# Attention and routed experts on one core: a new order for the swaps, the first pairs, the first plan and the last pairs

## The chip, the core and the metric

The kernel runs on one core of a Trainium2 chip. Its engines have queues of their own: TensorE (PE in the profile, its weight loads PEld), VectorE (DVE), ScalarE (ACT), GpSimd (POOL), and SyncE (SP), which here only issues transfers. Transfers run on the core's 16 DMA engines. The metric is the device time of one execution in microseconds (us), as the median of the runs. In the profile L230 is line 230 of the kernel.

## What is computed

Attention over 8 batches of 8 heads (576 tokens, 64 columns a head), with rotary positions on q and k, and behind it a layer of 8 experts in which each token goes to the one with the highest gate:

```python
q_rot, k_rot = (rotate(q), rotate(k))
scores = scale * np.matmul(q_rot, k_rot.transpose(0, 1, 3, 2))
attn = softmax(scores)
x = (attn @ v)                      # as (4608 tokens, 512)
...
logits = x @ w_gate + modality_bias[modality_id]
e_idx = np.argmax(logits, axis=1)
for e in range(8):
    mask = e_idx == e
    h = np.maximum(x[mask] @ w1[e], 0.0)
    out[mask] = gate_w[mask, None] * (h @ w2[e])
```

## The kernel before, in words

**Attention** goes by 32 pairs of heads, four pairs to a batch. The loop over the pairs (L734) doesn't emit work directly: each step is a job with a key (`KEYS`, in us within a pair's period `PER` = 14.438), jobs are sorted by key + `PER` x pair (L819), and each engine, SP too, runs its share strictly in that order. So a smaller key means an earlier place in an engine's queue, not a time. Negative keys belong to pairs ahead. The steps of a pair:

- LD (`load`, L139): q and k of the pair, with the rotated partner beside them, 1216 columns, into one of two stages `Rs`. SP issues it; it has to wait until the pair two before has been read by LO.
- T1, T2, R (`rope_` parts 0 to 2, L230, L232, L234): two products with the cosine and sine tables and their sum, on GpSimd for pairs from 2 on, on VectorE for pairs 0 and 1.
- HI (L221 by way of `acopy`, ScalarE) rounds the result to the matmul's type; LO (L238, GpSimd) is what rounding left. Each matmul of the scores runs as three: high x high, low x high, high x low.
- SWH and SWL (`swap`, L246): a copy of the high and of the low part, `SW`, in which the two heads have changed halves of the partitions; two transfers of 64 partitions each, so four a pair. SWH has its key behind HI, SWL behind LO.
- S0 to S8 (`scores`, L261), MN (`rowmin`, L270) and EX (`expo`, L277): score tiles on TensorE into a ring of three PSUM buffers, the row minimum on VectorE, the exponential on ScalarE into `PJ` and `P4`.
- F0 to FB (`fill`, L283; evacuated by `evac`, L315 or L221): transposes of the exponentials into `PH` and `PD`.
- AVA, AVB (L339), OUTA, OUTB (L370), EVA, EVB (L384 to L390): times V, back to rows of tokens with the gate's logits beside them, and division by the row sum.
- LV (`loadv`, L147, L148): V of the pair, four transfers.

The keys that matter here, from `KEYS`: T1 -32.78, T2 -26.38, R -23.03, HI -18.83, SWH -17.41, LO -15.27, SWL -11.79, LD -39.33, LV -10.14, S8 -5.22. Modulo the period this gives on GpSimd the order T1 of the next pair, LO of this one, T2 and R of the next; and on SP: SWL of a pair, LD of the pair two on, LV.

**Routing** comes once in four pairs, in 13 steps (`route`, keys `AT["rk"]`) over ScalarE, VectorE, GpSimd and TensorE. Then five scatters (`scatter`, L472, GpSimd's queue) write each token's number and weight to its rank in the table `TAB`; their keys lie 10.5 apart (9.0 in one batch). XO (L395, L399) writes the batch's rows to `X`.

**The first plan** (`plan(0)`, L479) runs after six batches, in 28 steps. From the counts so far it takes eight full blocks of 256 tokens with one expert each, so that the expert layer can start before the last two batches are routed. It works on one partition, on GpSimd, with its sums and one shift (L492) on VectorE.

**The experts** go by blocks (`chain`, L845): table rows (`m_ix`, L604, L606), gathers of X (L614, GpSimd), transposes (L655), weights W1 and W2 into `ST1` and `ST2` (L626, L631, SP; these are also the stages `Rs` and the tables), split into high and low parts (L218, L221), 96 matmuls for W1 (L673) and 48 for W2 (L690), and a scatter of the result (L694). For block 0 this work is put among the last pairs by keys counted from pair 31 (`Z`, L786 to L818). W2's two parts (`mw`, L825) and the experts' PSUM banks are allocated after attention's pools have been closed (L824), and wait for all of them.

**The start**: pair 0 comes in three pieces of columns, `FIRST` (L151): 0 to 416, 928 to 1216, 416 to 928. Each goes through all five steps of the rotation and its swaps before the next. Pair 1's load is issued behind them (L157), its rotation follows on VectorE, then the loads for pairs 2 and 3, V, and `setup2` (L202: the modality bias, on GpSimd). Only then do the sorted jobs begin.

## Time and profile before

| | us |
|---|---|
| median of 3 runs | 976.48 |
| lowest, highest | 976.05, 978.91 |
| the profiled execution | 978.22 |
| its span, first to last instruction | 976.4 |
| first score matmul | 14.86 |
| first matmul with W1 | 524.08 |
| first matmul with W2 | 550.96 |

The profile is one execution of the program. Its timelines give the start of an instruction, its length, engine, line, the tile that it writes and the ones that it reads, and in brackets how long the engine had been idle ahead of it and what ended that. Merged rows have a count behind an x. A row of SPq is the issue of a transfer, not the transfer. Windows give for a stretch its length and each engine's busy time; then the clock that TensorE was granted, the mean busy share of the DMA engines, and GB/s. The view of waits gives who waited for whom: us in total, how often, and the longest. Busy TensorE isn't TensorE at its best: matmuls overlap, and a slower clock makes them longer.

### The profile page before, as it was taken

The page shows a single profiled execution, that of the slowest core. Times are in us where ns is not written, and L with a number is a line of the kernel's source. Part 1 is how long each engine was busy: PE and PEld are TensorE (multiplying, and loading weights), DVE is VectorE, ACT ScalarE, POOL GpSimd, SP SyncE. Part 2 cuts the span into 40 slices and gives each one's busy share as a digit, 9 for nine tenths or more (in the row PEclk, how much of TensorE's full clock was granted, in tenths as well). Part 3 has the DMA queues.
Part 4 walks back from the last instruction along what each step waited for, and adds up shares of the span by engine and source line. Part 5 has one row for each costly group of instructions (what it writes and reads, how often), then busy time and mean ns, then how long its engine had stood idle before and what let it go on. Part 6 is the DMA issues. An engine that isn't in the chain of part 4 may idle for free. (4 is left out here: it accounts for less than half of the span.)

```text
span 976.4 us, 24969 instructions
## 1 busy us (share of the span) xinstructions
PE 908.2 (93%) x9248; PEld 742.4 (76%) x9248; DVE 674.2 (69%) x1158; ACT 632.3 (65%) x1299; POOL 663.8 (68%) x498
## 2 busy tenths in 40 slices
PE   1899999999999999989977899999999999999996
PEld 1677677777777767767646689999998888899995
DVE  6677777787777777777754478677666666666771
ACT  1778787787787877868753355666555656556661
POOL 7776788889878798799656076557666666556500
PEclk9799999999999999999989899999999999999998
DMA  9645667566574755746751261111431611611100
GB/s 285 194 142 173 180 198 221 148 188 202 174 225 134 201 185 175 228 130 182 207 149 34 64 211 36 55 48 58 142 120 42 218 38 45 227 44 49 41 24 15
DMA packets 71964, 132.71 MB, mean 136 GB/s; under 512 B 28395, under 2 KB 48267, under 8 KB 66844
## 3 DMA queue, kind: packets, MB, share of 16 engines
q1 hardware_dynamic: 61436, 110.32, 37.8%
q0 software_dynamic: 9536, 19.48, 6.4%
q8 instruction: 75, 1.23, 0.6%
q10 hardware_dynamic: 864, 1.25, 0.4%
q14 instruction: 53, 0.43, 0.2%
HBM read 140.59 MB, written 19.77 MB: 164 GB/s over the span
## 5 line engine op out<-in xcount | busy, mean ns | idle before, releaser
L270 DVE TENSOR_REDUCE mn<-ps 128x1 f32<-128x576 f32 x288 | 205.4, 744 | 104.2 <-PE ps L261 67.3
L277 ACT ACTIVATE P<-ps,mn 128x576 f32<-128x576 f32 x288 | 210.4, 737 | 97.6 <-DVE mn L270 90.4
L614 POOL DMA_INDIRECT XG<-X,iy x152 | 180.9, 1190 | 47.5 <-issue 41.4
L673 PE MATMUL psH<-HL,W1H 128*128 128x256 f32 x1152 | 202.7, 279 | 0.0
L261 PE MATMUL ps<-HL 64*128 64x288 f32 x960 | 170.7, 315 | 29.8 <-ACT HL L221 14.9
L261 PE MATMUL ps<-SW 64*128 64x288 f32 x960 | 170.3, 316 | 9.0 <-DMA SW<-HL 4.7
L261 PEld LDWEIGHTS ps<-HL 64*128 64x128 f32 x960 | 137.7, 190 | 53.2 <-ACT P L277 15.9
L673 PEld LDWEIGHTS psH<-HL,W1H 128*128 128x128 f32 x1152 | 176.8, 188 | 1.7
L673 PE MATMUL psH<-HL,W1L 128*128 128x256 f32 x576 | 160.8, 279 | 0.7 <-DVE W1L L218 0.7
L261 PEld LDWEIGHTS ps<-SW 64*128 64x128 f32 x960 | 135.4, 190 | 24.4 <-ACT P L277 14.1
L218 DVE TENSOR_TENSOR W1L<-ST,W1H 128x1024 fp32r<-128x1024 f32 x76 | 90.0, 1222 | 84.6 <-ACT W1H L221 82.6
L339 PE MATMUL pa<-PH,V 128*64 128x320 f32 (+1 forms) x1024 | 142.2, 420 | 1.1 <-PE ps L261 0.7
L694 POOL DMA_INDIRECT out_dram<-y,ix x38 | 39.1, 1030 | 143.6 <-ACT y L693 129.8
L690 PE MATMUL psY<-W2H,SW 128*128 128x512 f32 x304 | 120.3, 396 | 1.4 <-ACT W2H L221 1.4
L690 PE MATMUL psY<-W2L,SW 128*128 128x512 f32 x304 | 120.4, 396 | 0.4 <-DVE W2L L218 0.4
L283 PE MATMUL ps<-idf,P 64*128 64x64 f32 x2624 | 105.3, 229 | 8.8 <-DVE PH L315 2.4
L283 PEld LDWEIGHTS ps<-idf,P 64*128 64x128 f32 x2624 | 92.6, 141 | 22.7 <-ACT PH L221 8.6
L315 DVE COPY PH<-ps 128x512 f32<-128x512 f32 (+1 forms) x160 | 97.3, 632 | 17.4 <-PE ps L283 10.9
L339 PEld LDWEIGHTS pa<-PH,V 128*64 128x64 f32 x1024 | 69.8, 139 | 51.5 <-issue 14.5
L673 PEld LDWEIGHTS psH<-HL,W1L 128*128 128x128 f32 x576 | 108.2, 188 | 0.9 <-DVE W1L L218 0.9
L221 ACT ACTIVATE PH<-ps 128x512 f32<-128x512 f32 (+1 forms) x160 | 84.0, 556 | 22.1 <-PE ps L283 14.9
L218 DVE TENSOR_TENSOR W2L<-ST,W2H 128x1024 fp32r<-128x1024 f32 x76 | 92.4, 1220 | 4.1 <-ACT W2H L221 3.6
(159 smaller groups left out, 1602.9 us busy)
## 6 DMA issues: line engine op xcount, KB each, us to landing
ST<-in_moe_w_dram SPq DMA_DIRECT2D x152, 512.0 KB
ST<-in_qk_dram SPq DMA_DIRECT2D x31, 1216.0 KB
SW<-HL SPq DMA_DIRECT2D x124, 232.0 KB
V<-in_v_dram SPq DMA_DIRECT2D x64, 128.0 KB
X<-X SPq DMA_DIRECT2D x8, 1024.0 KB
XG<-X,iy POOLq DMA_INDIRECT x152
V<-in_v_dram SPq DMA_DIRECT2D x64, 16.0 KB
X<-XT SPq DMA_DIRECT2D x32, 32.0 KB
```

The costliest lines, as they stand in the source:

```text
L218: nc.vector.tensor_tensor(o, a, b, op=ALU.subtract)
L221: return nc.scalar.activation(o, i, AF.Copy, scale=scale)
L261: free(nc.tensor.matmul(ps[:, g, 0:288], t[:, wq, q0:q0 + P], t[:, wk, k0:k0 + 288], start=(m == 0), stop=(m == len(L) - 1)), seen)
L270: lastmin[d["ring", u]] = nc.vector.tensor_reduce(mn, d["S", u][:, :, 0:288], op=ALU.min, axis=AX.XY).ins
L277: nc.scalar.activation(p.rearrange("p (a b) -> p a b", a=2), ps[:, :, 0:288], AF.Exp, bias=d.pop(("m", u)), scale=-1.0, accum_out=d["sum"] ...
L283: free(nc.tensor.transpose(ps[0][:, g, c:c + 64], src[r, k0:k0 + P], idf[r, r]), ps[1])
L315: mine.append((nc.vector.tensor_copy if g else acopy)(o, i).ins)
L339: nc.tensor.matmul(pa[hh * 64:hh * 64 + 64, 0:c1 - c0], d["V"][:, hh, kt, :], r, start=(kt == 0), stop=(kt == 4))
L614: nc.gpsimd.indirect_dma_start(out=XG[s % 2][:, t, g, :], out_offset=None, in_=X.rearrange("n (i f) -> (n i) f", f=P)[0:rows], in_offset=b ...
L673: nc.tensor.matmul(ps[:, i, :], w[:, c, f0:f0 + P], x[:, c, :], start=(m == 0), stop=(m == 11))
L690: nc.tensor.matmul(ps, hx[:, c, t * P:(t + 1) * P], w[:, c, :], start=(m == 0), stop=(m == 23))
L694: nc.gpsimd.indirect_dma_start(out=out, out_offset=bass.IndirectOffsetOnAxis(ap=d["ix"][:, t, 0:1], axis=0), in_=y, in_offset=None, bounds ...
```

## The change

- `swap` sends both parts in one transfer, so there are two a pair, at SWL's key. SWH is no longer used. For pair 0 the second transfer of each piece goes out on ScalarE's queue.
- `FIRST` becomes 0 to 288, 672 to 1216, 288 to 672. The rotation of the three pieces is interleaved. The score tiles of pair 0 come in the order 8, 6, 7, 0 to 5; its evacuations follow their transposes directly, and AVA and AVB come directly behind the last transposes.
- Pair 1's load is issued behind the first piece's swap; its rotation runs on GpSimd, with HI, LO and the swap behind pair 0's transposes F3. Behind these come the load of pair 3 and T1, T2, R of pair 2. `setup2` goes to key 20.5.
- The route steps from the fourth on are moved later, up to 33.0. Scatters lie 2.5 apart and no longer wait for one another.
- `plan0`, a generator of nine steps, replaces `plan(0)`. It counts full blocks by comparisons and a sum, without the shift; sums on VectorE, the rest on GpSimd. It starts at the tenth route step.
- The first plan's table reads and the scatters of the last two batches no longer wait for each other.
- Block 0's side work has new keys. W2's parts take the places of `PJ` and `PH` as soon as these are done with, and are split during pair 31, not behind it. Pools of the experts wait by tile, not for all of attention.
- V's main parts of both heads come in one transfer. `y` and `BT` have places of their own.

```diff
 AT = dict(
-    rk=(0, 0.6, 1.5, 4.7, 5.5, 6.3, 6.9, 7.5, 9.6, 10.4, 11.2, 14.4, 15.2),
-    pl=1.5,
-    sc=(10.5, 9.0),
-    tr=3.5,
-    te=-8.0,
-    hi=(-14.0, -9.0, -5.0, -1.0),
+    rk=(0, 0.6, 1.5, 7.0, 8.5, 9.5, 10.0, 11.0, 24.0, 24.9, 25.6, 32.0, 33.0),
+    pl=(0.5, 6.5, 7.5, 13.5, 14.5, 20.5, 21.5, 28.5, 29.5),
+    sc=2.5,
+    plan=(-30.5, -21.0, -14.5, -13.0, 2.0, 4.0, 6.0, 8.0),
+    ix=(-19.7, -12.5, 0.0, 5.0),
+    rows=(-15.0, -4.0, 6.5),
+    gap=(1.35, 1.3, 1.3),
+    w1=(-29.3, -27.8, -23.2, -20.9),
+    w2=(-8.5, -6.5, -4.0, -1.5),
+    te=(-4.0, -2.0),
+    hi=(-14.0, -10.0, -6.0, 0.0),
+    hi2=(10.2, 11.4, 12.6, 13.8),
+    lo2=(17.0, 18.2, 20.8, 22.0),
     l1=(7.0, 10.0, 13.7, 17.6),
     l1e=3.0,
-    sp2=(0.2, 0.4, 1.4, 1.8),
-    l2=2.0,
-    w1=(1.0, 5.7, 8.0, 10.2),
-    w2=(-8.0, -5.0, -2.0, 1.0),
-    plan=(-99.0, -15.0, 4.0, 6.0, 8.0, 10.0, 12.0, 14.0),
-    ix=(-16.5, -9.5, 4.0, 6.0),
-    rows=4.0,
-    gap=1.3,
+    l2=0.1,
...
-    pp = att.enter_context(tc.tile_pool(name="pp", bufs=1))
+    pp = ctx.enter_context(tc.tile_pool(name="pp", bufs=1))
...
+    W2 = [None] * 2
+    places = [ExitStack(), ExitStack()]
+
+    def place(i, name, **kw):
+        return places[i].enter_context(tc.tile_pool(name=name, bufs=1, reuse_waits="tile", **(dict(side="right") if i == 0 else {}), **kw))
+
+    def weights2(i):
+        places[i].close()
+        W2[i] = ctx.enter_context(tc.tile_pool(name=f"w2{i}", bufs=1, reuse_waits="tile", **(dict(side="right") if i == 0 else {}))).tile(
...
+    pj = place(0, "pj")
+    PJ = [pj.tile([P, 2 * S], F32, name=f"P{j}") for j in range(4)]
...
     def loadv(n):
         b, hp = divmod(n, 4)
         V = Vs[n % 2]
+        nc.sync.dma_start(out=V[:, :, 0:4, :].rearrange("p h j d -> p h (j d)"),
+                          in_=v[b, 2 * hp:2 * hp + 2, 0:512, :].rearrange("h (p j) d -> p h (j d)", j=4))
         for hh in range(2):
-            src = v[b, 2 * hp + hh]
-            nc.sync.dma_start(out=V[:, hh, 0:4, :], in_=src[0:512, :].rearrange("(p j) d -> p j d", j=4))
-            nc.sync.dma_start(out=V[hh * 64:hh * 64 + 64, hh, 4, :], in_=src[512:576, :])
-
-
-    FIRST = ((0, 416), (K1, QW), (416, K1))
...
+    FIRST = ((0, Q0), (672, QW), (Q0, 672))
     st[0] = dict(R=Rs[0], HL=HL[0], SW=SW[0], V=Vs[0])
     for c0, c1 in FIRST:
         nc.sync.dma_start(out=Rs[0][:, :, c0:c1], in_=qk[0, :, :, c0:c1])
         nc.scalar.dma_start(out=COS[:, c0:c1], in_=rope[0, :, c0:c1])
         nc.scalar.dma_start(out=SIN[:, c0:c1], in_=rope[1, :, c0:c1])
...
-        BT = PJ[0][:, 0:B * 5 * E].rearrange("p (b e) -> p b e", e=E)
...
-        e = nc.vector if n < 2 else nc.gpsimd
...
-    def swap(n, i, c0=0, c1=QW):
+    def swap(n, c0=0, c1=QW, engs=None):
         d = st[n]
         a, b = (d[t].bitcast(F32) for t in ("SW", "HL"))
         for g in range(2):
             c = slice(max(c0, Q0 * g), min(c1, QW if g else K1))
             if c.start < c.stop:
-                nc.sync.dma_start(out=a[g * 64:g * 64 + 64, i, c], in_=b[64 - g * 64:128 - g * 64, i, c])
...
+    placed = []
+    taken = []
+
     def scatter(b, j):
         oi = bt_[b]["oi"]
         n = P if j < 4 else 64
-        nc.gpsimd.indirect_dma_start(
+        inst = nc.gpsimd.indirect_dma_start(
             out=TAB, out_offset=bass.IndirectOffsetOnAxis(ap=oi[0:n, j:j + 1], axis=0),
-            in_=VAL[0:n, b, j, :], in_offset=None, bounds_check=E * N - 1, oob_is_err=False)
+            in_=VAL[0:n, b, j, :], in_offset=None, bounds_check=E * N - 1, oob_is_err=False).ins
+
+        for _b, x in placed:
+            tc.declare_no_dep(inst, x, reason="rows of other tokens")
+        placed.append((b, inst))
+        if b >= B - 2:
+            for x in taken:
...
+    def plan0():
+        G_ = nc.gpsimd
...
+        def total(o, i):
+            nc.vector.tensor_reduce(o, i, op=ALU.add, axis=AX.X)
+
+        most = (B - 2) * S // BLK
+        sl = cview("SL")[0:1]
+        nf, nb, cum, ge, tk = (t1(x, [E]) for x in ("nf", "nb", "cum", "ge", "tk"))
+        G_.tensor_tensor(nf, RUN[0:1, B - 2, :], cview("EB")[0:1], op=ALU.subtract)
+        th = t1("th", [NB_MAX])[:, 0:most]
+        G_.tensor_scalar(th, sl[:, 0:most], float(BLK), float(BLK), op0=ALU.mult, op1=ALU.add)
+        full = t1("full", [E, NB_MAX])[:, :, 0:most]
+        sh = [1, E, most]
+        G_.tensor_tensor(full, nf.unsqueeze(2).to_broadcast(sh), th.unsqueeze(1).to_broadcast(sh), op=ALU.subtract)
+        G_.tensor_scalar(full, full, 0.0, None, op0=ALU.is_ge)
+        yield
+        total(nb, full)
+        t88 = t1("t88", [E, E])
+        G_.tensor_tensor(t88, cview("TRI")[0:1].rearrange("p (a b) -> p a b", b=E), nb.unsqueeze(1).to_broadcast([1, E, E]), op=ALU.mult)
+        yield
+        total(cum, t88)
+        yield
+        sh = [1, NA, E]
+        cmp = t1("cmp", [NB_MAX, E])[:, 0:NA, :]
+        G_.tensor_tensor(cmp, cum.unsqueeze(1).to_broadcast(sh), sl[:, 0:NA].unsqueeze(2).to_broadcast(sh), op=ALU.subtract)
+        G_.tensor_scalar(cmp, cmp, 0.0, None, op0=ALU.is_le)
+        es = t1("pes", [NB_MAX + 1])
+        G_.memset(es[:, 0:1], -1.0)
+        yield
+        total(es[:, 1:NA + 1], cmp)
+        yield
+        G_.tensor_scalar(es[:, 1:NA + 1], es[:, 1:NA + 1], float(E - 1), None, op0=ALU.min)
+        G_.tensor_copy(PLA[:, 0, 0:NA], es[:, 1:NA + 1])
...
+        G_.tensor_scalar(ge, nb, -float(BLK), float(N), op0=ALU.mult, op1=ALU.add)
+        G_.tensor_tensor(cmp, cmp, ge.unsqueeze(1).to_broadcast(sh), op=ALU.mult)
+        yield
+        rb = t1("rb", [NB_MAX])[:, 0:NA]
+        total(rb, cmp)
...
+        i1 = nc.sync.dma_start(out=ix, in_=TAB[bass.ds(d["r"], BLK), :].rearrange("(p t) w -> p t w", t=2)).ins
         xi = d["xi"] = ixp.tile([P, 8, 2], I32, name="xi", tag="xi")
-        nc.sync.dma_start(out=xi, in_=TAB[bass.ds(d["r"], BLK), :].rearrange("(q g) w -> q (g w)", g=8).unsqueeze(0).to_broadcast([4, 32, 16]))
+        i2 = nc.sync.dma_start(out=xi, in_=TAB[bass.ds(d["r"], BLK), :].rearrange("(q g) w -> q (g w)", g=8).unsqueeze(0).to_broadcast([4, 32, 16])).ins
+        if not slots[s][0]:
+            for i in (i1, i2):
+                for b, x in placed:
+                    if b >= B - 2:
+                        tc.declare_no_dep(i, x, reason="the first plan's blocks lie before the rows of the last two batches")
...
-    for n in range(2):
-        for c in FIRST if n == 0 else ((0, QW),):
-            for part in range(5):
-                rope_(n, part, *c)
-                if part > 2:
-                    swap(n, part - 3, *c)
-        load(n + 2)
-    for n in range(2):
-        loadv(n)
-    setup2()
+
+    for part, c in ((0, 0), (1, 0), (2, 0), (3, 0), (4, 0), (0, 1), (1, 1), (2, 1), (3, 1), (0, 2), (4, 1), (1, 2), (2, 2), (3, 2), (4, 2)):
+        rope_(0, part, *FIRST[c])
+        if part == 4:
+            swap(0, *FIRST[c], engs=(nc.sync, nc.scalar))
+        if (part, c) == (4, 0):
+            load(1)
+    loadv(0)
+    load(2)
+    loadv(1)
+    for part in range(3):
+        rope_(1, part)
     z = NPAIR - 1
     end = max(K["EVA"], K["EVB"]) + 0.015
     r0 = end + 0.005
+
+    places_ = sorted(range(9), key=lambda u: K[f"S{u}"])
+    first = (8, 6, 7, 0, 1, 2, 3, 4, 5)
+    OV = {0: {}, 1: {}, 2: {}}
+    for nm in ("S", "MN", "EX"):
+        OV[0].update({f"{nm}{u}": K[f"{nm}{w}"] for u, w in zip(first, places_)})
+    full = max(K[f] for f in K if f[0] in "SF") + 0.05
+    assert full + 0.3 < min(K[f"S{u}"] for u in range(9)) + PER
+    for f in ("F0", "F1", "F2", "F3", "FA", "FB"):
+        OV[0].update({f"{e}_{f}": K[f] + 0.01 for e in "AB"})
+    OV[0].update(AVA=full + 0.01, AVB=full + 0.02)
+    for i, nm in enumerate(("HI", "LO", "SWL")):
+        OV[1][nm] = K["F3"] + 0.02 + 0.01 * i - PER
+    for i, nm in enumerate(("T1", "T2", "R")):
+        OV[2][nm] = K["F3"] + 0.1 + 0.01 * i - 2 * PER
+    J(K["F3"] + 0.06, "load", 0, load, 3)
...
+        if n > 0:
+            for part, nm in enumerate(("T1", "T2", "R", "HI", "LO")):
+                if n > 1 or part > 2:
+                    K_(nm, rope_, n, part)
+            K_("SWL", swap, n)
         if n > 1:
-            for part, nm in enumerate(("T1", "T2", "R", "HI", "LO")):
-                K_(nm, rope_, n, part)
-            for i in range(2):
...
+            if n == NPAIR - 9:
+                g = plan0()
+                for i in range(9):
+                    J(r0 + AT["rk"][9] + AT["pl"][i], "plan", n, next, g, None)
             for j, (f, *a) in enumerate(scats):
...
+    for s in range(NA):
+        Z(A["plan"][s], m_plan, s)
+    for s in range(4):
+        Z(A["ix"][s], m_ix, s)
+    for s in range(3):
+        for i in range(8):
+            Z(A["rows"][s] + A["gap"][s] * i, m_gather, s, i // 4, i % 4)
...
+        Z(A["w1"][g], m_load1, 0, g)
+        Z(A["w2"][g], m_load2, 0, g)
+        Z(A["hi"][g], m_hi, 0, g)
+        Z(A["hi"][g] + 1.3, m_lo, 0, g)
+        if g == 0:
+            for i in range(2):
+                Z((A["hi2"], A["lo2"])[i][0] - 0.01, weights2, i)
+        Z(A["hi2"][g], m_hi, 1, g)
+        Z(A["lo2"][g], m_lo, 1, g)
+    for t in range(2):
+        Z(A["te"][t] - 0.5, m_tr, 0, t)
...
-        Z(end + A["sp2"][g], m_split, 1, g)
...
-    mw = ctx.enter_context(tc.tile_pool(name="mw", bufs=1))
-    W2[0] = mw.tile([P, 8, DM], F32R, name="W2H")
-    W2[1] = mw.tile([P, 8, DM], F32R, name="W2L")
-    W2[2] = ctx.enter_context(tc.tile_pool(name="my", bufs=2))
     for kind, nb in (("H", 4), ("Y", 4)):
-        banks[kind] = ctx.enter_context(tc.tile_pool(name=f"ps{kind}", bufs=nb, space=PSUM))
```

More of the change, by code (lines that the diff above doesn't have):

```diff
@@ L483, in t1, with plan @@
+    def plan():
+        V_ = nc.vector
+        pl, ns = PLB, NB_MAX
         def t1(name, sh, dt=F32):
@@ L765, in tile_attention_moe @@
             g = route(n // 4)
-            early = n == NPAIR - 9
             r1 = r0 + AT["rk"][-1] + 0.02
@@ L813, in tile_attention_moe @@
-    for g in range(4):
-        l1 = max(A["l1"][g], A["hi"][g] + 1.5, w1_ + 11.5, te_[1] + 1.5, max(K[f] for f in K if f[0] in "SF") + 0.1 * g + 0.1)
+    planned = r0 + AT["rk"][9] + AT["pl"][-1] - 8 * PER
+    assert A["ix"][0] > r1 + 4 * AT["sc"] - 8 * PER
+    fills = max(K[f] for f in K if f[0] in "SF")
+    assert A["plan"][0] > planned and A["ix"][0] > planned and A["w1"][0] > max(K["T1"], K["LO"] - PER)
+    assert A["w2"][0] > max(K["T2"], K["LO"]) and A["te"][0] > max(K[f"S{u}"] for u in range(9)) - PER
```

126 lines of the change are left out of this document (52 added, 74 removed).

## The prediction

> **What bounds the kernel now.** I read the page first, then the stages by windows, then the timeline of single queues. The page's row of TensorE over 40 slices of the span, busy tenths in each:
>
> ```profile
> PE   1899999999999999989977899999999999999996
> ```
>
> TensorE is the bound nearly everywhere, and what it loses lies in the first slice and in slices 21 to 23, where attention hands over to the experts. Windows by stage (length, busy time of each engine, granted clock, DMA share, GB/s): one attention pair, the handover, and a block of the experts.
>
> ```profile
> 53.27:67.88 14.61, 14.45 (x205) 10.82 (x203) 10.90 (x24) 11.55 (x32) 11.17 (x5) 1.00 0.57 173
> 496.07:550.96 54.89, 40.91 (x359) 29.86 (x359) 22.86 (x46) 20.60 (x46) 27.42 (x28) 0.84 0.29 74
> 573.80:598.70 24.90, 24.90 (x164) 22.54 (x163) 17.41 (x25) 14.12 (x18) 16.85 (x16) 1.00 0.33 112
> ```
>
> The expert block is full, as are its neighbours in the row of slices: nothing is to be had there, and the change leaves them alone. In attention a pair takes 14.6 us where nothing disturbs it, and TensorE is busy for 14.45 of them. So a second loop matters, one that is only just hidden: GpSimd and SP at work on the rotation. GpSimd's timeline for one turn, then SP's:
>
> ```profile
> 190.26 2.79 POOL L238 TENSOR_TENSOR HL<-ST,HL 128x1216 fp32r<-128x1216 f32 x1
> 193.00 2.78 POOL L232 TENSOR_TENSOR ST<-ST 128x1216 f32<-128x1216 f32 x1
> ...
> 200.81 2.80 POOL L230 TENSOR_TENSOR ST<-ST 128x1216 f32<-128x1216 f32 x1 [1.06 <-DMA ST<-in_qk_dram]
> 203.55 2.81 POOL L238 TENSOR_TENSOR HL<-ST,HL 128x1216 fp32r<-128x1216 f32 x1
> ```
>
> ```profile
> 188.41 5.76 SPq L246 DMA_DIRECT2D SW<-HL  x4
> 194.23 0.57 SPq L139 DMA_DIRECT2D ST<-in_qk_dram  x1
> ```
>
> LO (L238) of one pair ends at 193.0; SP then sends the low half's swap and the load two pairs on (LD, 194.23); T1 (L230) of that load waits for it; the next LO stands behind that T1. From LO to LO that is 203.55 - 190.26 = 13.3 us, against TensorE's 14.6. T1 waits for its load 25 times, as the view of waits says; in an undisturbed pair LO in the end waits 1.2 us for ScalarE:
>
> ```profile
> POOL ST L230 <- DMA ST<-in_qk_dram: 51.1, 25, 3.9
> ```
>
> ```profile
> 53.21 2.78 POOL L238 TENSOR_TENSOR HL<-ST,HL 128x1216 fp32r<-128x1216 f32 x1 [1.21 <-ACT HL L221]
> ```
>
> So the loop's slack is 14.6 - 13.3 = 1.3 us.
>
> **The change, part by part.** Times are of the profiled execution: 978.2 us, of which its span is 976.4; the median of the runs shown is 976.48, so I add differences to 976.5.
>
> *One transfer for both halves of a swap.* It removes two of four SP issues for each pair. But the high half, so far sent while LO still ran, now goes with the low half after LO, and LD stands behind both in the same queue. The high half alone, in one-microsecond windows:
>
> ```profile
> 189.00:190.00 1.00, 1.00 (x14) 0.64 (x12) 0.87 (x2) 1.00 (x5) 1.00 (x1) 1.00 0.50 112
> 190.00:191.00 1.00, 1.00 (x12) 0.61 (x10) 0.00 (x0) 1.00 (x4) 1.00 (x2) 1.00 0.94 215
> 191.00:192.00 1.00, 1.00 (x18) 0.83 (x16) 0.32 (x1) 0.07 (x1) 1.00 (x1) 1.00 0.54 177
> ...
> 195.00:196.00 1.00, 1.00 (x18) 0.95 (x16) 0.50 (x1) 0.80 (x3) 0.84 (x2) 1.00 0.99 299
> ...
> 197.00:198.00 1.00, 1.00 (x26) 0.80 (x24) 1.00 (x4) 1.00 (x5) 1.00 (x1) 1.00 1.08 428
> ```
>
> The shares of the first three rows add up to 0.50 + 0.94 + 0.54 = 1.98, so a half (128 rows of 928 floats, 475 KB) takes 2.0 us of all sixteen engines. At 299 GB/s it would take 1.6, at 428 (the load's best row) 1.1; nothing if the load could pass it. I take 1.8, near its own rows. The loop becomes 13.3 + 1.8 = 15.1 us, longer than TensorE's 14.6: **GpSimd, SP and the queue become the bound of attention**.
>
> A rule speaks for the transfer. The Trainium skill, "DMA: Bandwidth & Descriptors", section "Where 436 GB/s comes from", says that the fabric's ceiling, 435 GB/s, is what binds SBUF to SBUF transfers. By that, an estimate, a half costs 1.1 us, and 13.3 + 1.1 = 14.4 stays under 14.6. The rows of this case show 215 GB/s at a share of 0.94; the rule's outcome is rival A.
>
> *Scatters 2.5 us apart, not 10.5.* Five per batch. Before, one fell into each pair; one directly behind LO delays the load:
>
> ```profile
> 144.53 2.79 POOL L238 TENSOR_TENSOR HL<-ST,HL 128x1216 fp32r<-128x1216 f32 x1
> 147.46 1.00 POOL L472 DMA_INDIRECT TAB<-VAL,oi  x1
> ...
> 156.91 2.79 POOL L230 TENSOR_TENSOR ST<-ST,ST 128x1216 f32<-128x1216 f32 x1 [2.77 <-DMA ST<-in_qk_dram]
> ```
>
> Here T1 comes 9.6 us after LO's end (147.3), against 200.81 - 193.0 = 7.8: 1.8 us for one scatter. Now four of the five lie between one LO and the next T1, the fifth between T1 and LO, where it costs its 1.0 outright. For the four I take 3.0 (bounds 0.6, GpSimd's time alone, and 5.4, three whole delays). The step after the logits (L423 to L426) also stays between T1 and LO:
>
> ```profile
> 402.54 0.26 POOL L423 TENSOR_TENSOR dl<-lg,mx 128x40 f32<-128x40 f32 x1
> ...
> 403.52 2.77 POOL L238 TENSOR_TENSOR HL<-ST,HL 128x1216 fp32r<-128x1216 f32 x1
> ```
>
> 1.0 us. Together 5.0 for a routed batch (2.6 to 7.4). The other route steps are spread out; what their closeness cost TensorE before no longer counts where GpSimd sets the pace.
>
> *First plan.* Its shift on VectorE goes:
>
> ```profile
> 420.72 2.72 DVE L492 TENSOR_SCALAR ni<-ni 1x8 int32<-1x8 int32 x1 [0.76 <-POOL ni L490]
> ```
>
> A shift of 8 numbers took 2.72 us there. Its successor's GpSimd steps fall where GpSimd waits for a load (the 1.06 at 200.81, 2.8 more in the longer loop); without that cover they would cost their own time, once. A gain on VectorE is worth nothing in a loop-bound attention; I count 0.
>
> *Edits with one answer.* V's two main transfers become one: the same bytes, still behind LD. The y tiles and the bias scratch get places of their own: no operation more or less. All 0; were V ahead of LD, its 288 KB would cost about 1 us a pair at the rates above.
>
> From LO's end in pair 3 (53.21 + 2.78 = 56.0) to that in pair 30 (470.5, below) it took 414.5 us. After: 27 turns x 15.1 + 7 batches x 5.0 = 442.7: **+28.2**.
>
> *The start.* The first minima stand behind VectorE's work for pair 1, which goes to GpSimd:
>
> ```profile
> 21.38 1.85 DVE L238 TENSOR_TENSOR HL<-ST,HL 128x1216 fp32r<-128x1216 f32 x1 [1.28 <-ACT HL L221]
> ```
>
> ```profile
> 20.13 1.22 ACT L221 ACTIVATE HL<-ST 128x1216 fp32r<-128x1216 f32 x1 [5.33 <-DVE ST L234]
> 23.94 0.74 ACT L277 ACTIVATE P<-ps,mn 128x576 f32<-128x576 f32 x1 [2.59 <-DVE mn L270]
> ...
> 31.84 0.74 ACT L277 ACTIVATE P<-ps,mn 128x576 f32<-128x576 f32 x1
> ```
>
> ```profile
> 16.42 0.52 POOL L205 CAST MF<-MI 128x40 f32<-128x40 int32 x1 [2.71 <-DMA MI<-in_moe_modality_id_dram]
> ...
> 23.33 0.18 POOL L214 COPY RUN<-CF 128x8 f32<-128x8 f32 x1
> ```
>
> The first exponential waits for its minimum until 23.94, and that for VectorE's LO. In the new order two pieces suffice for the first three score tiles. I put the first exponential at 17 (not before 14.8, when ScalarE is through with pair 0's last piece, 20.13 - 5.33; not after 23.9). Pair 1's load now stands behind the first piece's swap; with three GpSimd steps of 2.8 from about 14 on, its rotation is ready at 22.5, 3 us before it is needed. For pair 1's HI stands behind the eighth exponential: 17 + 8.6 = 25.6, plus 1.2, plus LO's 2.8 gives 29.6. From there the loop runs: LO of pair 2 ends at 44.7. In the next turn the bias setup (16.42 to 23.51, so 7.1 us, some of it beside VectorE; I take 5.8) has to fit into the gap between the end of that turn's rotation (two steps, 5.5 us after LO) and T1 at 7.8 + 1.8 = 9.6, which is 4.1: LO of pair 3 ends at 44.7 + 15.1 + 1.7 = 61.5 instead of 56.0. **+5.5**: the early scores are lost, for LO is what is late next.
>
> *The handover.* A row of SP's view of waits, then rows of GpSimd and TensorE:
>
> ```profile
> SPq L604 <- DMA TAB<-VAL,oi: 55.7, 4, 23.6
> ```
>
> ```profile
> 470.48 2.78 POOL L232 TENSOR_TENSOR ST<-ST 128x1216 f32<-128x1216 f32 x1
> ```
>
> ```profile
> 496.07 0.37 PE L261 MATMUL ps<-HL 64*128 64x288 f32 x1 [0.66 <-DVE PH L315]
> ```
>
> ```profile
> 550.96 0.47 PE L690 MATMUL psY<-W2H,SW 128*128 128x512 f32 x1 [1.41 <-ACT W2H L221]
> ```
>
> The table reads wait for scatters, the last swap and the gathers stand behind them, and W2's split waits for attention's pools. The change takes these waits away. Before, 80.5 us pass from LO's end in pair 30 (470.5) to the first W2 matmul. After: the swap lands at +5.6 (1.2 to the issue, 4.0 for two halves, 0.4 to be seen), plus 3.1 for two W1 loads (1.05 MB at some 340 GB/s) that now stand ahead of it on SP; 14.6 for pair 30; from pair 31's first score on, TensorE's 40.91 us at a clock of 0.84 are 34.4 at full clock; 3 for what stays. 8.7 + 14.6 + 34.4 + 3 = 60.7: **-19.8**.
>
> Sum: 5.5 + 28.2 - 19.8 = +13.9. **Forecast: 990 us.** Its own range is 978 to 1004, from the bounds of the batch term (+-17), and of handover and start (+-6).
>
> **The rivals.**
>
> A, faster: the second half is hidden, TensorE keeps the pace. For it: the load's 428 GB/s. Against: FIFO, 215 GB/s. It decides below 1.3 us per half. 27 x 14.6 + 7 x 0.5, an allowance for routing, = 397.7 is -16.8; start -1; handover -19.8: 939 us.
>
> B, faster: the loop binds, but bunched scatters overlap. For it: four small ones may share one slow stretch. A batch costs 1.6 then: 27 x 15.1 + 11.2 = 418.9 is +4.4; with +5.5 and -19.8: 966.5. It turns at 3 us a batch, where the sum is 976.
>
> C, slower still: the handover keeps its waits, in another shape. ScalarE's 11.55 us a pair get ten more operations in pairs 30 and 31, four of them W2's, and VectorE as many; or the early table reads still wait for scatters (the change not doing what it says). For it: both engines ran two thirds full already. Against: from 496 on TensorE idles or crawls for 20 of 55 us, which leaves room. It decides once those queues run behind TensorE by more than the 3 us allowed. 8 instead of 19.8: 1002.
>
> **How the numbers follow.** Forecast 0.42, A 0.17, B 0.28, C 0.13. About 0.3% (3 us) is what can be told from no change. Slower: 0.41 + 0.12 = 0.53; within: 0.08, mostly of B's edge; faster: 0.39. The range 944 to 1004 leaves out half of A and a little of C.
>
> **What would show it.** LO to LO on GpSimd near 15.1 us in pairs without scatters, T1 at 9.6 after LO's end, TensorE waiting for SW at the first score tile of most pairs, and LO of pair 30 ending near 504. If instead T1 comes at 8 after LO and TensorE's pairs take 14.6, A holds; if batches with scatters take no more than 2 us over, B. The first W2 matmul 61 us after LO of pair 30 would show the handover term. The prediction is wrong if the second half does not delay the load.

## The result: slower by 5.7%, four times the loss that was forecast

The changed kernel took 1033.6 us (median of 4 runs, 1030.2 to 1037.7), the kernel before, beside it, 977.7; the ratio is 1.057 (1.052 to 1.062). Forecast was 990, with a range up to 1004. The sign was right, the size was not. The profiled execution has a span of 1032.3 us against 976.4.

The page of the changed kernel, TensorE's row over 40 slices; then two rows of its view of waits (total us, times, longest):

```profile
PE   2799898888887989889987899999999999999996
```

```profile
POOL ST L243 <- DMA ST<-in_qk_dram: 93.5, 24, 5.6
...
PE ps L274 <- DMA SW<-HL: 58.4, 24, 7.5
```

From slice 5 to slice 21 eights, and one seven, stand in most places where nines stood. T1, now L243, waits for its load 93.5 us in all instead of 51.1, and TensorE waits 24 times for a swap at a pair's first score tile. GpSimd's timeline shows one turn after another; LO is now L251:

```profile
183.93 2.79 POOL L251 TENSOR_TENSOR HL<-ST,HL 128x1216 fp32r<-128x1216 f32 x1
...
196.40 2.79 POOL L243 TENSOR_TENSOR ST<-ST 128x1216 f32<-128x1216 f32 x1 [3.33 <-DMA ST<-in_qk_dram]
...
199.29 2.78 POOL L251 TENSOR_TENSOR HL<-ST,HL 128x1216 fp32r<-128x1216 f32 x1
...
215.75 2.81 POOL L251 TENSOR_TENSOR HL<-ST,HL 128x1216 fp32r<-128x1216 f32 x1
...
232.21 2.77 POOL L243 TENSOR_TENSOR ST<-ST 128x1216 f32<-128x1216 f32 x1 [2.98 <-DMA ST<-in_qk_dram]
...
236.09 2.79 POOL L251 TENSOR_TENSOR HL<-ST,HL 128x1216 fp32r<-128x1216 f32 x1
```

Three turns, LO to LO: 15.4, 16.5 and 20.3 us. The first is the quietest of all; the last has the scatters of a batch in it. Where the forecast's sum was taken, LO of pair 3 to LO of pair 30, and on to the first W2 matmul:

```profile
64.26 2.78 POOL L251 TENSOR_TENSOR HL<-ST,HL 128x1216 fp32r<-128x1216 f32 x1
...
535.84 2.78 POOL L251 TENSOR_TENSOR HL<-ST,HL 128x1216 fp32r<-128x1216 f32 x1
```

```profile
606.30 0.50 PE L758 MATMUL psY<-W2H,SW 128*128 128x512 f32 x1
```

| stretch, us | before | forecast | after | forecast's change | measured change |
|---|---|---|---|---|---|
| start to LO(3)'s end | 56.0 | 61.5 | 67.0 | +5.5 | +11.0 |
| LO(3) to LO(30), 27 turns | 414.5 | 442.7 | 471.6 | +28.2 | +57.1 |
| LO(30) to the first W2 matmul | 80.5 | 60.7 | 67.7 | -19.8 | -12.8 |
| from there to the end | 425.4 | as before | 426.0 | 0 | +0.6 |

All three terms erred to the same side. The 27 turns, LO's end to LO's end, worked out from the timeline (those of about 20 us have a batch's scatters in them):

```
16.3 15.6 17.5 16.6 15.5 20.7 17.6 15.4 16.5 20.3 16.6 17.0 16.5 21.8
17.5 16.4 16.8 20.4 16.7 16.9 16.6 19.9 17.7 15.6 16.3 20.3 16.9
```

### The profile page after: what moved, and what is told of

The parts are those of the page before. It is cut to its first block, busy times and chain, and to the rows that moved or that the text cites. A ratio compares the mean times of both kernels' runs of the same rounds, so it can differ in the third digit from the quotient of the medians.

```text
span 1032.3 us, 24793 instructions
## 1 busy us (share of the span) xinstructions
PE 927.1 (90%) x9248; PEld 756.5 (73%) x9248; DVE 667.0 (65%) x1154; ACT 635.3 (62%) x1299; POOL 673.7 (65%) x503
## 5 line engine op out<-in xcount | busy, mean ns | idle before, releaser
L274 PEld LDWEIGHTS ps<-SW 64*128 64x128 f32 x960 | 141.3, 203 | 83.0 <-DMA SW<-HL 63.8
L274 PE MATMUL ps<-HL 64*128 64x288 f32 x960 | 177.1, 326 | 15.8 <-ACT HL L234 11.6
L274 PEld LDWEIGHTS ps<-HL 64*128 64x128 f32 x960 | 142.3, 202 | 34.9 <-issue 15.5
L352 PE MATMUL pa<-PH,V 128*64 128x320 f32 (+1 forms) x1024 | 152.1, 444 | 1.1 <-DVE PH L328 1.1
L352 PEld LDWEIGHTS pa<-PH,V 128*64 128x64 f32 x1024 | 74.4, 150 | 57.8 <-issue 23.9
L296 PE MATMUL ps<-idf,P 64*128 64x64 f32 x2624 | 105.2, 230 | 11.5 <-ACT PH L234 2.5
L251 POOL TENSOR_TENSOR HL<-ST,HL 128x1216 fp32r<-128x1216 f32 x31 | 86.3, 2784 | 9.3 <-ACT HL L234 9.2
```

What stands on the lines that cost most here:

```text
L251: e.tensor_tensor(d["HL"][:, 1, c], a, d["HL"][:, 0, c].bitcast(F32), op=ALU.subtract)
L274: free(nc.tensor.matmul(ps[:, g, 0:288], t[:, wq, q0:q0 + P], t[:, wk, k0:k0 + 288], start=(m == 0), stop=(m == len(L) - 1)), seen)
L296: free(nc.tensor.transpose(ps[0][:, g, c:c + 64], src[r, k0:k0 + P], idf[r, r]), ps[1])
L352: nc.tensor.matmul(pa[hh * 64:hh * 64 + 64, 0:c1 - c0], d["V"][:, hh, kt, :], r, start=(kt == 0), stop=(kt == 4))
```

## The experiments

Two theories stood at first. **Q, the queue:** the high half, behind LO and ahead of the load, makes the loop LO, swap, load, T1 longer than TensorE's pair. **S, the scatters:** their bunching costs, the swap hardly. The sets ran on different chips, so each ratio is against the kernel before beside it. "27 pairs" is the time between the first products with V of pairs 2 and 29 on TensorE's timeline: 413.6 before, 475.5 after. "Handover" is from that of pair 29 to the first W2 matmul: 69.5 and 54.1. The 26 pairs from 2 to 28, where needed, leave out the turn before pair 29, into which the changed kernel moves work for W1.

| run | ratio (95%) | 27 pairs | handover |
|---|---|---|---|
| e1 high half early again | 1.011 (1.003 to 1.020) | 416.0 | 74.6 |
| e2 load ahead of the swap | 1.075 (1.065 to 1.085) | 477.9 | 80.0 |
| e3 scatters 9.0 apart | 1.065 (1.056 to 1.074) | 473.7 | 76.4 |
| e4 before, with the merged swap only | 1.053 (1.043 to 1.063) | 474.7 | 71.7 |
| e5 two halves, both after HI | 0.996 (0.993 to 0.999) | 412.4 | 53.9 |
| e6 early half, pair 1's load later | 0.992 (0.989 to 0.995) | 412.1 | 53.8 |
| e7 the same, SP's order in the handover | 0.990 (0.983 to 0.996) | 403.6 | 55.7 |
| e8 before, beside e5 to e7 | | 414.4 | 61.7 |
| e9 two halves, both behind LO | 1.066 (1.059 to 1.073) | 463.7 | 75.7 |
| e10 half of the high half early | 1.028 (1.021 to 1.035) | 427.2 | 74.3 |
| e11 e7, pair 1's HI behind the exponentials | 1.009 (1.003 to 1.015) | 410.3 | 77.6 |
| e12 e11, pair 1's load at the very start | 1.016 (1.009 to 1.023) | 409.1 | 82.8 |
| e13 the changed kernel again | 1.078 (1.068 to 1.087) | 470.7 | 78.5 |
| e14 e7 again | 1.014 (1.004 to 1.024) | 408.4 | 83.1 |
| e15 e7, third block's gathers later | 1.015 (1.007 to 1.022) | 410.3 | 71.3 |
| e16 before, beside e13 to e15 | | 414.5 | 71.6 |
| e17 e1 with an extra transfer ahead of the load | 1.072 (1.067 to 1.077) | 489.6 | 53.2 |
| e18 e1 with scatters 9.0 apart | 0.997 (0.995 to 1.000) | 412.2 | 54.2 |

### Is it the merged swap?

The high half alone back in its place:

```diff
...
-            K_("SWL", swap, n)
+            K_("SWH", swap, n, 0, QW, None, slice(0, 1))
+            K_("SWL", swap, n, 0, QW, None, slice(1, 2))
```

> The changed kernel, but from pair 1 on each swap goes in two transfers again, the high half while LO still runs. Theory Q (the high half stands ahead of the load in SP's queue, and so sets T1 and the turn of GpSimd's loop): quiet pairs come back to TensorE's 14.6 us, turns with the logits' step to about 15.3, turns with scatters from 20.6 to 18.4; 27 turns take 14 x 14.7 + 7 x 15.3 + 6 x 18.4 = 423 us instead of 472, so the time falls from 1034 to about 985 us. Rival S (the scatters 2.5 us apart and code packets that fall into the load are what costs; the half's place costs only the 0.35 us by which the quietest turn is over 15.1): about 27 x 0.35 = 10 us are gained, 1024 us.

And the kernel before with nothing but the merge (`K_("SWL", swap, n, slice(0, 2))` in place of the two calls):

> The kernel before with nothing but the merged swap from pair 2 on, behind LO. Theory Q: GpSimd's loop becomes the bound of attention there too, with turns of 15.5 to 16.5 us instead of a mean of 15.35 with all delays; 27 turns gain some 23 to 45 us: 1000 to 1023 us, 1012 the likeliest. Rival S (the merge alone is hidden or nearly so; what costs is its meeting with the bunched scatters): 977 to 985 us.

Undone, the merge gives back the whole loss of attention, 475.5 to 416.0; done alone, it makes it, 474.7. T1's waits fall from 93.5 us to this row of e1:

```profile
POOL ST L243 <- DMA ST<-in_qk_dram: 31.9, 16, 3.2
```

Scatters, still bunched in e1, cost TensorE next to nothing. S falls as far as attention goes. Q said 985 us for e1, 1.007 of 977.7; 1.011 was measured. For e4 it said at most 1023, 1.046; 1.053 was measured.

### Is it the place in the queue, or the form of the transfer?

The first attempt, with SWH's key just ahead of SWL's:

> The changed kernel, from pair 1 on with two transfers for each swap again, but both behind LO, directly one after the other. Theory Q (what costs is that the high half waits for LO and then stands ahead of the load; one transfer or two is the same): as slow as the changed kernel, or some us more for two more issues: 1.055 to 1.085 of the kernel before. Rival D (the form of the merged transfer costs, two pieces a row instead of one): back to the level of the run with the early high half, 1.01 of the kernel before.

It gave 0.996, the level of rival D. But it had not done what its text says. SP's timeline:

```profile
195.30 4.78 SPq L259 DMA_DIRECT2D SW<-HL  x4
200.13 0.58 SPq L153 DMA_DIRECT2D ST<-in_qk_dram  x1
```

The four issues stretch over 4.8 us: the high half went out as soon as HI was through, and only the low half stood waiting for LO. A place in the queue holds nothing back that nothing stands ahead of. So the low half was put first (`"SWH": -11.78`, behind SWL's -11.79):

> The changed kernel, from pair 1 on with two transfers for each swap, the low half first, so that the high half really waits behind it for LO (in the run with late halves it stood ahead of the low half and went out as soon as HI was through). Theory Q (place in the queue): T1 comes 9.6 to 11 us after LO's end again, and the time is that of the changed kernel, 1.05 to 1.08 of the kernel before. Rival D (the merged form): 1.00.

```profile
198.36 2.80 POOL L251 TENSOR_TENSOR HL<-ST,HL 128x1216 fp32r<-128x1216 f32 x1
211.44 2.76 POOL L243 TENSOR_TENSOR ST<-ST,ST 128x1216 f32<-128x1216 f32 x1 [4.48 <-DMA ST<-in_qk_dram]
```

```profile
201.19 2.48 SPq L259 DMA_DIRECT2D SW<-HL  x4
203.72 0.58 SPq L153 DMA_DIRECT2D ST<-in_qk_dram  x1
```

Now all four go behind LO (it ended at 201.2), T1 comes 10.3 us after it, and most of the loss is back: 463.7 us, 1.066. One transfer or two makes no such difference; what stands between LO and the load does. (The merged form took 470.7 to 475.5 us, in e13 and the changed kernel; where those 7 to 12 us come from was not tried.) How much of it:

```diff
...
-            K_("SWL", swap, n)
+            K_("SWH", swap, n, 0, QW, None, slice(0, 1), (0,))
+            K_("SWL", swap, n, 0, QW, None, slice(1, 2), (0,))
+            K_("SWL", swap, n, 0, QW, None, slice(0, 2), (1,))
```

> The changed kernel, with half of the high half sent early (partitions 0 to 63 of the swap) and the other half of it with the low half behind LO. Theory Q, with its threshold: the loop's turn becomes 13.3 + 1.1 = 14.4 us, just under TensorE's 14.6, so quiet pairs keep 14.6 and only turns with scatters and the logits' step lengthen, by up to 1.1 us in 13 turns: 1.00 to 1.015 of the kernel before. A cost in proportion to what stands ahead of the load: half of the changed kernel's 5.7%, 1.025 to 1.03.

The ratio of 1.028 is that of the proportional cost, but the pairs say otherwise. On that chip the 26 pairs from 2 to 28 took 394.8 us with the high half early (e11), 402.9 with half of it behind LO, 439.7 with all (e9): 8 us for the first half, 37 for the second. (The 27 pairs of the table can't be compared here: e11 also has e7's order for W1's loads, and its turn from pair 28 to 29 took 15.6 us, against 24.3 in e10.) It bends, as with Q's threshold; in e10's turns without scatters or the logits' step T1 came 8.5 to 9.8 us after LO, and the turns took 14.5 on average. The rest of the ratio lies at the ends: pair 2's product with V came at 75.6 us, against 68 to 69 in the kernel before, and the turn from 28 to 29 (24.3 us against some 17) and the handover (74.3) are long.

### The load, or the landing of the swap?

> The changed kernel, with the merged swap kept, but SP sends the load of two pairs on (LD) ahead of the swap. Theory Q: the loop from LO through LD to T1 loses the swap's 4 us and more; T1 comes about 6 us after LO's end, a turn of the loop is 6 + 5.6 = 11.6 us, under TensorE's 14.6, so quiet pairs take 14.6 and scatter turns about 16.5: 21 x 14.6 + 6 x 16.5 = 406 us instead of 472, the time about 967 us. Rival W (what binds is the way from LO through the swap to the next scores, and the swap now lands 4 us later): no gain or some us more, 1030 to 1045 us. Rival S (scatters): scatter turns stay near 20, 21 x 14.6 + 6 x 20 = 427 us, the time about 988 us.

The edit is `"LD": -41.0`. T1 then came about 7 us after LO in the turns that didn't wait for route steps, and the kernel was no faster: 477.9 us for the 27 pairs, and 1.075, where e3, with the load behind the swap, had 1.065 on the same chip (the intervals overlap). That is rival W. In the quiet pairs TensorE did come down to 14.6 to 16 us, but where it waited for the swap it now went on 11.6 us after LO's end, against 6.7 in the changed kernel (medians). Of GpSimd's view of waits:

```profile
POOL dl L436 <- DVE mx L433: 47.3, 8, 8.8
POOL rk L471 <- DVE RUN L469: 41.5, 6, 7.7
```

The same two rows had 3.4 and 0.6 us in the changed kernel. GpSimd stands at route steps that wait for VectorE, which waits for TensorE (141.5 us at the row minima), which waits for the swap; and the next LO stands behind these steps. That is another loop, through the late swap. The merge could cost by either, so the load alone was made late:

```diff
...
+            if 1 < n < 30:
+                K_("SWL", again, n)
```

`again` copies the low half once more, from HL into a tile that nothing reads.

> The kernel with the early high half; in pairs 2 to 29 a transfer of the size of the high half, into a tile that nothing reads, stands between the low half and the load. The swap lands when it did (3.2 us after LO's end), the load comes some 2 us later. If the load's place is what costs (loop from LO through the load to T1): 27 pairs take 460 to 475 us instead of 412 to 416. If the swap's landing is what costs: 412 to 420 us.

```profile
207.25 2.13 SPq L259 DMA_DIRECT2D SW<-HL  x2
209.43 1.23 SPq L268 DMA_DIRECT2D DUM<-HL  x2
210.71 0.62 SPq L153 DMA_DIRECT2D ST<-in_qk_dram  x1
```

```profile
POOL ST L243 <- DMA ST<-in_qk_dram: 119.8, 27, 6.8
```

The swap is early, the load is late, and 27 pairs take 489.6 us, over even the upper bound of 475. (By the packet records the next pair's high half runs beside the load here, which it cannot in the merged kernel; the load itself takes 5.1 to 6.1 us in turns without scatters, in e1 3.5 to 4.5.) So a late load is enough for the loss; a late swap, as e2 shows, costs in its own way in turns with route steps.

### The scatters

> The changed kernel with the five scatters of a batch 9.0 apart in the order instead of 2.5. Theory Q: each scatter costs the bound loop its own 1.0 us and one in five 1.8 more, 5.8 us a batch, as much as the 5.1 measured for the bunch: 1030 to 1038 us. Rival S (it is the bunching that costs): a spread scatter is hidden, the six turns of 20.6 us fall to about 16.5, 25 us less: about 1009 us.

> The kernel with the early high half, its scatters 9.0 apart in the order instead of 2.5. Theory Q: where the loop has slack, neither spacing costs TensorE much: 27 pairs take 412 to 418 us, and T1 of the turn behind a scatter comes at 9.6, not at 10.7 to 12. Rival S: the bunch costs some us a batch here too, and the spread is 10 us or more faster.

Spread scatters in the bound loop: 473.7 against 475.5 us, no difference, as Q had it. In the loop with slack: 412.2 against 412.4 to 416.0, none either. The spacing matters in neither; a batch's scatters cost the bound loop much the same wherever they stand. (T1 came 7.7 to 11.3 us after LO in e18's turns with scatters; 9.6 was expected.) What e3's ratio is over that of the changed kernel lies in its handover.

### The start

```diff
...
-        if (part, c) == (4, 0):
-            load(1)
+    load(1)
     loadv(0)
```

> The kernel with the early high half, and pair 1's load behind the swaps of pair 0's last piece. Theory L (that load, 1.2 MB ahead of them in the DMA engines, holds the last swaps until 19.7 us): the first exponential comes at 17 to 18 us instead of 22.3, LO of pair 1 ends 3 to 5 us earlier, and the time falls by 4 us, to 1.007 of the kernel before. Rival (pair 1's rotation becomes late instead): no gain, 1.01 or more.

The first exponential, in e5 (with the load where the change has it) and in e6:

```profile
21.55 0.74 ACT L290 ACTIVATE P<-ps,mn 128x576 f32<-128x576 f32 x1 [8.16 <-DVE mn L283]
```

```profile
19.86 0.74 ACT L290 ACTIVATE P<-ps,mn 128x576 f32<-128x576 f32 x1 [6.69 <-DVE mn L283]
```

It comes 1.7 us earlier, and the kernel takes 2.3 us less, 966.0 against 968.3 (the intervals of the ratios overlap). Less than the 4 us expected: pair 1's rotation gets later, as the rival said (T1 at 22.2 us instead of 17.0). And the load was not all that held up the scores: in e6 the second piece's swap, issued from 11.6 us on, still ended only at 16.3 by the packet records. Two attempts to win more:

> The fastest version so far (early high half, pair 1's load behind pair 0's swaps, W1 loads and second table read behind the swaps), with HI, LO and swap of pair 1 behind pair 0's last exponential instead of ahead of it. That exponential waited there for a rotation that ended at 30.26 us; it comes some 2 us earlier, and so do the transposes: 2 us less than the run with the order changed, 0.987 of the kernel before. Rival (pair 1's own scores set the pace at the start): no gain.

> The same, with pair 1's load issued directly behind pair 0's loads instead of behind its swaps. Theory L, taken on: it is through before the swaps start at 11.7 us, GpSimd's T1 of pair 1 starts near 13 instead of 21.9 us, and pair 1's HI no longer waits: 2 to 4 us less than the run before this one. Rival (it slows pair 0's tables and the last pieces of its rotation): no gain or some us lost.

Neither did. In e11 pair 0's product with V comes 1.1 us earlier than in e7, but pair 1's at 59.5 us, against 58.5 in e7 and 60.6 in e14, the same program on another chip. In e12 the early load holds up pair 0's own tables: VectorE waits 2.4 us for the last piece's. Then its two next steps for that piece took 2.28 and 3.01 us instead of 0.55 and 0.56 in e7:

```profile
14.78 2.28 DVE L246 TENSOR_TENSOR ST<-ST,ST 128x384 f32<-128x384 f32 x1 [0.73 <-DMA ST<-in_rope_dram]
17.10 3.01 DVE L248 TENSOR_TENSOR ST<-ST 128x384 f32<-128x384 f32 x1
```

GpSimd's rotation of pair 1, early too, ran beside them (13.65 to 22.7 us); in e7 it began at 21.9, when they were through. So ScalarE's HI for pair 0's last piece ran in e12 at

```profile
20.14 0.52 ACT L235 ACTIVATE HL<-ST 128x384 fp32r<-128x384 f32 x1 [9.04 <-DVE ST L248]
```

against 12.8 in e7, and pair 0's product with V at 41.7 against 36.3: the rival. Every order with pair 1's rotation on GpSimd reached pair 2's product with V 4 to 15 us later than the kernel before, at 73 to 83 us against 68 to 69.

### The handover

W1's first loads and the second table read behind the swaps, `w1=(-26.0, -25.4, ...)`, `ix=(-19.7, -11.5, ...)`:

> The same, and in the handover the first two W1 loads stand behind pair 30's swap on SP, and the second table read behind pair 31's. If SP's order is what the handover loses: pair 30's swap lands some 3 us earlier and the time falls by 3 to 4 us against the run before this one. Rival (VectorE's extra steps, and the instructions that TensorE lacks while GpSimd gathers, set the end of the handover): no difference between the two.

> The kernel before, unchanged, for a profile on this chip. If the pauses of TensorE between 527 and 544 us that the run with the early high half showed belong to the handover as both kernels have it, they are here too, with some 86 to 97 us from the first product with V of pair 28 to the first W2 matmul; if they come from the change, it is 86 us without them.

3.7 us were won (966.0 to 962.3), as expected, though the intervals overlap; by the profiles the gain lies in the turn from pair 28 to pair 29, 23.5 to 16.0 us. e7 is faster than the kernel before there, 0.990. From pair 28's product with V to the first W2 matmul, e8 took 78.7 us, less than either answer expected, and its view of waits has none of the pauses that the expectation asks about. But in e1 to e3 and in e9 to e12 the last pair alone took 38 to 41 us, against 23.5 in the changed kernel's profile. Kernel or chip?

> The changed kernel, unchanged, beside the others of this set on one chip. If the pauses of TensorE belong to the chip, the last pair takes about 40 us here too whenever it does so in the next run, and 23 whenever not; the ratio to the kernel before is then 1.06 to 1.07 with them and 1.057 without. If they belong to the kernels with the early high half, it takes 23 us here whatever the next run shows.

> The fastest version again. Theory chip: on a chip without the pauses 0.99 of the kernel before, on one with them 1.00 to 1.01, with 40 us for the last pair. Theory kernel: 0.99 and 25 us everywhere.

> The fastest version, with the eight gathers of the third block's rows 15.5 later in the order, behind the last scatters instead of between them. If the gathers cause the pauses: the last pair takes 15 us less than in the run before this one where that shows 40 us, and the time falls by as much. If the pauses are absent on this chip, or come from elsewhere: the same as the run before, within 0.3%.

> The kernel before, unchanged, for its handover on this chip: 78 to 80 us from the first product with V of pair 28 to the first W2 matmul if this chip shows no pauses, 86 or more if it does.

The last pair, from product with V to product with V, first of e7 on its first chip, then of e14, the same program on this one, by windows:

```profile
494.40:519.90 25.50, 20.35 (x228) 15.84 (x226) 15.40 (x30) 15.45 (x35) 19.10 (x20) 0.87 0.41 86
```

```profile
515.50:554.10 38.60, 25.89 (x228) 19.36 (x226) 15.19 (x30) 15.32 (x35) 18.07 (x19) 0.73 0.20 22
```

The same instructions, 13 us apart. e14's wait view and timeline show what fills them:

```profile
PE ps L296 <- issue: 17.5, 23, 2.5
```

```profile
529.48 0.35 PE L296 MATMUL ps<-idf,P 64*128 64x64 f32 x4 [0.37 <-issue]
530.22 0.34 PE L296 MATMUL ps<-idf,P 64*128 64x64 f32 x4 [0.39 <-issue]
```

TensorE gets its transposes four at a time, 0.7 us apart, and waits for nothing that the profile names; the granted clock of the stretch is 0.73 instead of 0.87. e13 has this too (last pair 39.9 us, ratio 1.078, over the 1.06 to 1.07 expected): it comes and goes with the chip or the occasion, not with the early half. The kernel before has such pauses too, and they cost it less. From pair 28's product with V to the first W2 matmul it took 88.5 us in e16 against 78.7 in e8; counted so, the changed handover turns from 1 to 7 us of gain (e5 to e7 against e8) into 10 or 11 of loss (e13 and e14 against e16). Moving the gathers away (e15) made the profile's handover 12 us shorter (71.3) and its last pair 4 us (34.5, not the 15 less that the gathers alone would explain), but left the time as it was, 993.4 against 994.3: what causes the pauses stays open.

## Why the prediction was wrong in size

**The bound moves to GpSimd, SP and the queue: right.** e1, e4, e9 and e17 show it. Rival A is out: the second half was not hidden. Both halves, and one half in the kernel before, by windows (length first, DMA share and GB/s last):

```profile
203.37:207.36 3.99, 3.38 (x85) 2.94 (x82) 3.64 (x11) 3.65 (x10) 3.91 (x2) 1.00 1.00 226
207.36:212.38 5.02, 4.79 (x71) 3.71 (x66) 4.47 (x11) 4.10 (x12) 0.53 (x2) 1.00 0.90 319
```

```profile
194.18:195.99 1.81, 1.81 (x24) 1.28 (x20) 0.49 (x1) 1.62 (x5) 1.65 (x2) 1.00 1.03 266
```

A half more costs 3.99 - 1.81 = 2.2 us; the forecast took 1.8. The Trainium skill's ceiling ("DMA: Bandwidth & Descriptors", section "Where 436 GB/s comes from") isn't reached: the engines are full, share 1.00, at 226 GB/s. So the rule's outcome, rival A, didn't come.

**The turn: the step that failed.** The forecast took the undisturbed turn, 15.1 us, for every turn without route work, and said that delays which cost TensorE before "no longer count" where GpSimd sets the pace. The quietest turn was 15.4, with T1 at 9.7 us, as foreseen. But the 14 turns without scatters or the logits' step took 16.3 on average, with T1 at 10.7, and in the turns with the logits' step T1 came at 10.7 as well. A loop with 1.3 us of slack swallows small delays of its load (in e1, T1 of such turns came 7.6 to 8.8 us after LO, and TensorE's quiet pairs still took 14.6); without slack each is paid. That is 27 x 1.17 = 31.6 us, more than the whole miss of this stretch. The forecast's range had no bound on this term, and 978 to 1004 is narrower than the +-17 and +-6 that it names would make it.

One of the small delays can be named from the trace, though no run tried it by itself. The second row of the fence above is a load of 5.02 us; the turn before had one of 4.0. The views of DMA of these two loads (queue: packets, MB, share):

```profile
q1 hardware_dynamic: 405, 1.53, 98.9%
...
q1 hardware_dynamic: 573, 1.59, 87.8%
q8 instruction: 1, 0.02, 1.3%
q14 instruction: 2, 0.02, 0.7%
```

In the first, only the queue of the loads was at work; in the second, three packets of program code came in between. One of them, of 16 KB, took 1.09 us by the packet records, and the last three rows of the load then ended one by one, 0.4 us apart, as on a single engine. By the packet records, loads without scatters took 5.0 us where such a packet fell into them or just ahead (13 of them), 4.2 where not (10). Of the 14 turns above, the 10 with such a packet took 16.6 us on average, the 4 without 15.5; in e13, the same program on another chip, it was 16.6 (12 turns) and 15.6 (2). So about 0.4 of the 1.2 us goes with the half itself, 2.2 instead of 1.8, and the rest came with these packets. In e1 they fell into 7 of 21 such loads and lengthened them less, 4.4 us against 4.2; why they came oftener and cost more in the changed kernel stays open. The Trainium skill ("Runtime: NRT & Kernel Launch", section "Instruction fetch mechanics") has code come in blocks of 16 KiB, at a cost mostly hidden; the size agrees for the larger packets here (others had 8 KB), and hidden it is only while the load has slack.

**The batch term: right in size.** Turns with the logits' step took 17.2, those with scatters 20.6. Over the 16.3 of the others that is 0.9 and 4.3, together 5.2 a batch (forecast 5.0). A seventh batch that I counted has its scatters behind pair 30, so 7 x 0.94 + 6 x 4.29 = 32.3 us instead of 35.0. With the 31.6 above that is the 28.9 us by which the loop was off. Rival B, overlapping scatters at 1.6 a batch, is out. That 2.5 or 9.0 apart is the same (e3) was not foreseen; the forecast priced the bunch as such.

**The start: half of it missed.** The forecast had pair 1's load behind the first swap, and looked only at pair 1. It overlooked that the load stands ahead of pair 0's other swaps. SP's, TensorE's and ScalarE's rows after the change:

```profile
8.26 0.60 SPq L153 DMA_DIRECT2D ST<-in_qk_dram  x1
12.30 2.80 SPq L259 DMA_DIRECT2D SW<-HL  x2
```

```profile
19.70 0.61 PE L274 MATMUL ps<-SW 64*128 64x288 f32 x1 [7.52 <-DMA SW<-HL]
```

```profile
22.33 0.74 ACT L290 ACTIVATE P<-ps,mn 128x576 f32<-128x576 f32 x1 [8.44 <-DVE mn L283]
```

The first exponential came at 22.3, not 17: 5.3 of the missing 5.5 us. e6, with the load out of the way, won a part of that back (19.9); the rest is the swaps' own landing, for which the forecast had no term.

**The handover: right in kind, 7 us short, and that with luck.** From LO(30) to pair 30's first full score tile took 10.5 us (forecast 8.7), pair 30 then 20.7 instead of 14.6, the rest 36.6 (37.4):

```profile
549.07:569.72 20.65, 18.22 (x227) 13.69 (x227) 14.75 (x29) 13.22 (x31) 12.52 (x14) 0.89 0.76 224
```

The forecast gave pair 30 an undisturbed pair's time. But at full clock TensorE's 18.2 us of work there would be 16.2 (18.22 x 0.89, an estimate), against 14.45 in an undisturbed pair; the clock was 0.89; and near the end TensorE waited twice for VectorE, 1.9 us in all, which had W1's splits and the rows' transposes to do:

```profile
563.00:575.00 12.00, 8.02 (x134) 6.05 (x128) 10.81 (x23) 7.23 (x18) 7.18 (x8) 1.00 0.70 225
```

VectorE was busy for 10.8 of 12 us there, TensorE for 8.0. That is rival C's mechanism at part of its price; with the pauses of other chips it comes true in full, for a reason that the forecast did not have.

The luck lies in the kernel before. The profile that the forecast was made from has pauses itself, behind pair 31's product with V: W1's matmuls come one to three at a time, and the view of waits has 3.8 us of `issue` ahead of them. e8's has none there. That stretch, up to the first W2 matmul, in the one and in the other:

```profile
529.88:550.96 21.08, 15.82 (x110) 10.87 (x109) 4.05 (x11) 4.42 (x8) 6.93 (x7) 0.84 0.12 19
```

```profile
531.22:545.13 13.91, 12.51 (x110) 9.53 (x109) 4.04 (x11) 4.52 (x8) 7.00 (x7) 1.00 0.19 29
```

From LO(30) to the first W2 matmul e8 took 72.9 us, not 80.5. Against that the changed kernel's 67.7 is a gain of 5.2 us, a quarter of the forecast's 19.8; some 7 of the 12.8 measured are pauses, which the changed kernel's profile doesn't have.

## What to carry to other kernels

Taking a transfer out of a list of issues saves nothing if what it is merged with leaves later: look at what stands behind it in the same queue, and whether a loop runs through that. And if a change uses up the slack of a hidden loop, don't price the loop at its quietest turn: every small delay that the slack swallowed is then paid, each turn. Here, by an estimate from the 14 quiet turns (0.74 us a turn), they came to some 20 of the 57 us that the 27 turns lost.

## What the hardware showed that I had not expected

The same program takes 25.5 us for its last pair on one chip and 38.6 on another, with TensorE's instructions coming four at a time, every 0.7 us, beside GpSimd's gathers; the profile names no cause. So a gain at such a place has to be measured on more than one chip: e7 is 0.990 (0.983 to 0.996) of the kernel before on one and, as e14, 1.014 (1.004 to 1.024) on another, where the kernel before itself ran between 976.6 and 996.2 us. Of the versions with the early half only this one was tried on two chips.

And VectorE's steps of 0.55 us took 2.3 to 3.0 us while GpSimd worked on a tile of its own beside them (e12; no run tried this by itself). Before work moves from one to the other, that is worth a look.
